# Hash-bucket attention and a feed-forward block: the hand-written order of 1185 steps is remade

## The chip, the cores and the metric

The kernel runs on one core of one Trainium2 chip. The metric is device time in microseconds (us) of one execution; where several runs are given, the median counts. A profiled execution has a time of its own, and inside it a span, from the first to the last instruction that the profiler saw.

## The reference

Inputs are q, k, v of shape (4 batches, 8 heads, 768 rows, 64), a projection of 64 x 6, a gain of 512, and two weight matrices, 512 x 2048 and 2048 x 512.

```python
q_bits = einsum('bhsd,dk->bhsk', q, proj) > 0      # k_bits likewise: 6 bits a row
mask   = q_bucket[:, :, :, None] == k_bucket[:, :, None, :]
scores = where(mask, q @ k.T / 8, -1e9)
attn   = softmax(scores);  a = attn @ v
x      = a with heads side by side                 # (4, 768, 512)
xn     = (x - mean) / sqrt(var + 1e-6) * g_ln
out    = x + relu(xn @ w_ch1) @ w_ch2
```

A row whose bucket no key shares takes the mean of v.

## The kernel before

**Tiles.** The 4 x 768 rows are cut into 12 units of 256 query rows (u = 0 to 11, three to a batch). A batch's 8 heads are two groups of four (g = 0, 1). A score step `S` (line 558) takes one unit, one group and one third of the keys (256 keys), so there are 72 steps s = 6u + 3g + third. A group's four heads lie at partitions 0, 32, 64, 96. Mask and scores are one accumulation: hash bits as +-0.5 are multiplied first (operand `G`), then q and k (`qb`, `kb`).

**What a step does.** `S.t.s` issues 24 matmuls on TensorE (PE) into two PSUM tiles `sc`, `E.a.s.0` and `E.a.s.1` (line 575) are the two exponentials on ScalarE (ACT), and `A.t.s` (line 587) multiplies their result with v and a column of ones into `acc`. `na`, `nb`, `nc`, `ag` on VectorE (DVE) turn `acc` into normalised rows and their mean and variance; `rs` on GpSimd (POOL) takes the root; `ce` centres; `fl` (line 638) transposes the rows by a DMA that SyncE (SP) issues. `F.t.u.p` (line 654) is one eighth of the first feed-forward product, `R` its relu on ACT or DVE, `P` (line 717) one of the seven products of a Strassen scheme for the second one, with its sums `ss` on DVE, `Y` adds a product to the rows and `O` stores a quarter of a unit.

**The first batch** (b = 0) has a path of its own, so as to start early. `lx` (line 370) loads a slab of q or k as it lies in memory. `tn.v.g.t.kp` (line 375, by `turn`, line 298) transposes one third kp of tensor t (0 is q, 1 is k) of group g; `ca` casts it to bf16; `ha.t.g.t.kp` (line 392) multiplies it in fp32 with the spread projection `pfull`, and `bh` (line 396) takes the signs into `G`. Thirds that aren't wanted at once take the way `hc`, `bc`, `sl`, `bi`. `lv` loads v, `cv` casts it into `vaug`, `sq` sums it and `sc` copies the sum. Unit 0 has no DMA transpose: `ft` transposes on PE and `fc` brings it out with the gain.

**Later batches** load with `LX` (line 507, after a one-column memset `gx` on POOL that holds the place), transpose with `tu`, cast with `CA`, hash with `hm` (line 521), take signs with `bt`, and go to DRAM and back (`mw` line 543, `mr` line 546) to reach the layout of `G`.

**Weights.** `lw1.p.n` (line 445) and `lw2.p.n` (line 456), n = 0 to 3, load a quarter of a weight matrix each, with a cast on the way, issued by POOL. `wg` multiplies the gain in for units from 1 on, `sw` forms Strassen's sums of weights.

**Warming.** `warm` (line 360) is 8 products of ones with ones, 512 columns each, into a PSUM tile of their own; `wm.t.0` to `wm.t.7` (line 365) are 8 more, one at a time, in the same tile. Nothing reads them.

**The order.** Nothing is scheduled by a compiler. `ORDER` (lines 16 to 136) lists 1185 words `name.engine.arguments`, and the loop at line 756 issues them as they stand. Each engine runs its own words strictly in that order; words of different engines meet only where one needs data or a buffer of another. The engine letter (v, a, p, s, t) says who does the step. `SLOTS` (lines 139 to 163) gives each tile its buffer by the order in which tiles are first named: `pp` has three double banks of PSUM for the pairs of `sc`, for `acc` and for the warming tile, `f` has two banks for everything else.

```python
for word in ORDER.split():
    name, eng, *args = word.split(".")
    OPS[name](ENGINES[eng], *map(int, args))
```

Of the kernel before, what the change touches and what calls it, by code (L numbers as in the profile page):

```python
# [21 lines left out]
tn.v.1.1.0 S.t.1.2 E.a.1.1 tn.v.1.0.0 ha.t.1.1.1 bh.v.1.1.1 cv.p.0.0.0 tn.v.1.1.2 gx.p.1.0.0 S.t.2.2  # L22
cv.p.0.0.2 cv.p.0.4.2 ca.p.1.1.2 E.a.1.0 ca.a.1.0.0 lv.s.1.0.3 lw1.p.1 ha.t.1.0.0 bh.v.1.0.0 gx.p.1.0.1
LX.s.1.0.0 ha.t.1.1.2 bh.v.1.1.2 E.a.2.1 lw1.p.0 ca.v.1.1.0 LX.s.1.0.1 tn.v.0.0.1 S.t.4.2 E.a.2.0
lv.s.1.0.2 ca.v.0.0.1 E.a.4.1 ha.t.1.1.0 A.t.0.2 A.t.2.2 sq.t.0.0 E.a.4.0 bh.v.1.1.0 S.t.3.2
sc.v.0.0 A.t.1.2 cv.a.0.4.0 E.a.3.1 hc.t.0.0.1 E.a.3.0 lw2.p.0 na.v.0.0 S.t.5.2 bc.v.0.0.1
sl.t.0.0.1 bi.v.0.0.1 E.a.5.1 sq.t.0.4 tn.v.1.0.1 S.t.8.2 hc.t.1.0.1 nb.v.0.0 nc.v.0.0 E.a.5.0
bc.v.1.0.1 E.a.8.0 A.t.4.2 A.t.5.2 sc.v.0.4 A.t.3.2 na.v.0.1 nb.v.0.1 E.a.8.1 sl.t.1.0.1
ca.a.1.0.1 bi.a.1.0.1 S.t.6.2 gt.t E.a.6.0 nc.v.0.1 ag.v.0.1 S.t.7.2 ag.v.0.0 ce.v.0.1
ft.t.0.1 ce.v.0.0 gc.v E.a.6.1 E.a.7.0 ft.t.0.0 S.t.9.2 E.a.7.1 E.a.9.0 fc.v.0.1  # L30
E.a.9.1 fc.v.0.0 F.t.0.3 A.t.7.2 R.a.0.3 F.t.0.7 R.a.0.7 S.t.10.2 tn.v.1.0.2 E.a.10.0
tu.v.1.0.1.2 gx.p.1.1.0 LX.s.1.1.0 lw1.p.2 tu.v.1.0.1.3 tu.v.1.0.0.3 lv.s.1.0.1 E.a.10.1 tn.v.0.0.2 hc.t.0.0.2
ca.a.0.0.2 tu.v.1.0.1.0 A.t.6.2 bc.v.0.0.2 sl.t.0.0.2 F.t.0.6 R.a.0.6 lw2.p.3 A.t.8.2 bi.v.0.0.2
# [24 lines left out]
A.t.25.2 O.s.1.0 R.a.2.6 nb.v.3.1 nc.v.3.1 F.t.2.4 nc.v.3.0 A.t.24.2 ag.v.3.0 su.p.2.0
A.t.26.2 na.v.4.0 E.a.29.1 LX.s.2.1.0 S.t.28.2 E.a.28.1 E.a.28.0 R.v.2.4 ag.v.3.1 hm.t.2.0
# [82 lines left out]
    E="012302132023132032103230103231032031230120302123031230120321013202120320",  # L142
# [646 lines left out]
```

## Time and profile before

| what | us |
|---|---|
| median of 3 runs | 295.62 (294.36 to 295.92) |
| the profiled execution | 294.86 |
| its span | 293.2 |
| DVE busy, mean of one relu (line 669) | 0.681 |
| ACT busy, mean of one relu (line 667) | 0.598 |
| first score matmul | 8.91 |
| last matmul ends | 288.9 |

The page gives, for each engine, its busy time; then the span in 40 slices; then the chain of work that ended last; then groups of equal instructions as `line engine operation out<-in xcount | busy, mean ns | idle before, what ended it`. A row of a timeline is `start us, length us, engine line operation out<-in xcount [idle before <-what ended it]`; rows with a count are runs of the same instruction. A row of the waits is `engine line <- what released it: us in total, times, longest`.

### The profile page before, as it was taken

Reading aid. Unit: us, or ns where it says so; the run is one execution under the profiler, and the core shown is the slowest. Engines: PE = TensorE matmul, PEld = TensorE weight load, DVE = VectorE, ACT = ScalarE, POOL = GpSimd, SP = SyncE. Lnnn points to the kernel's source line nnn. Section 1 sums busy time; section 2 is a strip of 40 time slices with the busy share of each in tenths; the row PEclk is TensorE's granted clock in tenths of the full one; section 3 lists DMA queues with packets and bytes.
Section 4 is the critical chain, followed back from the end, with each engine's and each line's share of the span. In section 5 each row is a group of like instructions: output and inputs, shape, how many; then the busy total and the mean of one; then the engine's idle time right before and its main releaser. Section 6 shows DMA issues by size and latency. Waiting matters only on the chain.

```text
span 293.2 us, 10524 instructions
## 1 busy us (share of the span) xinstructions
PE 285.6 (97%) x4650; PEld 227.7 (78%) x4650; DVE 206.8 (71%) x474; ACT 206.2 (70%) x236; POOL 54.0 (18%) x88
## 2 busy tenths in 40 slices
PE   8999999999999999999999999999999999999994
PEld 4677778648788887878778778877888878897883
DVE  4757899996769795797667995866666654773433
ACT  4689999998966978784865896887793694515240
POOL 5261325222423005000300107210010010000000
PEclk9999999999999999999999999999999999999999
DMA  6999997747744692362330352230410402304022
GB/s 223 302 319 250 216 277 133 139 134 171 174 122 131 134 307 76 127 189 51 98 82 1 83 132 63 60 61 3 92 37 2 74 2 52 78 6 104 2 72 73
DMA packets 31055, 34.10 MB, mean 116 GB/s; under 512 B 15521, under 2 KB 27809, under 8 KB 31010
## 3 DMA queue, kind: packets, MB, share of 16 engines
q1 hardware_dynamic: 25938, 28.72, 35.6%
q0 software_dynamic: 4224, 4.19, 8.9%
q8 instruction: 36, 0.59, 0.9%
q10 hardware_dynamic: 848, 0.53, 0.7%
q14 instruction: 9, 0.07, 0.1%
HBM read 27.86 MB, written 6.88 MB: 118 GB/s over the span
## 4 chain that ended last, share of the span: by engine, by line
PE 91%; DMA 3%; DVE 2%; SPq 1%; ACT 1%; issue 0%; ACTq 0%; DVEq 0%
PE f L659 27%; PE sc L570 18%; PE X L725 13%; PE acc L595 12%; PE Yb L725 7%; PE hp L526 3%; PE Ya L725 3%; PE hf L394 3%; PE f L674 2%; PE warm L363 1%; ACT E L576 1%; DMA G<-Bd 1%; DMA Bd<-B 1%; PE warm L366 1%; DMA xnT<-xc 1%; SPq L547 1%
## 5 line engine op out<-in xcount | busy, mean ns | idle before, releaser
L576 ACT ACTIVATE E<-sc,bias_sb 128x1024 bf16<-128x1024 f32 x144 | 153.1, 1111 | 36.0 <-PE sc L570 32.6
L659 PE MATMUL f<-xnT,w_sb 128*128 128x256 bf16 x768 | 94.2, 273 | 0.7 <-DMA xnT<-xc 0.6
L659 PEld LDWEIGHTS <-w_sb 128*128 128x128 bf16 x768 | 71.4, 98 | 13.6 <-issue 5.7
L667 ACT ACTIVATE hb<-f 128x512 bf16<-128x512 f32 x67 | 39.6, 598 | 34.5 <-PE f L659 34.5
L570 PE MATMUL sc<-qb,kb 32*128 32x256 bf16 x1152 | 52.5, 267 | 0.0
L595 PEld LDWEIGHTS <-E 128*128 128x128 bf16 x1152 | 40.8, 98 | 4.0 <-issue 2.5
L595 PE MATMUL acc<-vaug,E 128*128 128x65 bf16 x1152 | 43.7, 194 | 0.1
L570 PE MATMUL sc<-G 6*128 6x256 bf16 (+1 forms) x576 | 42.7, 273 | 1.1 <-ACT E L576 0.8
L725 PEld LDWEIGHTS <-hb 128*128 128x128 bf16 x352 | 33.4, 98 | 5.4 <-issue 1.3
L570 PEld LDWEIGHTS <-kb 32*128 32x128 bf16 x1152 | 30.5, 93 | 1.5
L635 POOL TENSOR_SCALAR rs<-mv 128x2 f32<-128x2 f32 x12 | 3.3, 277 | 150.4 <-DVE mv L624 150.4
L730 DVE TENSOR_TENSOR x<-X,x 128x256 f32<-128x256 f32 x44 | 18.4, 419 | 16.5 <-PE X L725 16.3
L570 PEld LDWEIGHTS <-G 6*128 6x128 bf16 (+1 forms) x576 | 16.0, 91 | 16.7 <-issue 13.3
L725 PEld LDWEIGHTS <-S 128*128 128x128 bf16 x264 | 25.0, 98 | 4.8 <-issue 1.4
L669 DVE TENSOR_SCALAR hb<-f 128x512 bf16<-128x512 f32 x29 | 19.7, 681 | 12.0 <-PE f L659 11.8
L304 DVE STREAM_TRANSPOSE T<-X 128x384 f32<-128x384 f32 (+2 forms) x52 | 26.1, 535 | 0.0
L725 PE MATMUL Yb<-w_sb,S 128*128 128x256 bf16 x176 | 22.9, 273 | 0.0
L608 DVE SCALAR_TENSOR_TENSOR y<-vsB,acc 128x520 f32<-128x520 f32 x24 | 16.5, 689 | 8.1 <-PE acc L595 7.8
L725 PE MATMUL X<-wt,hb 128*128 128x256 bf16 x168 | 21.8, 273 | 0.0
L617 DVE TENSOR_TENSOR x<-y,rc 128x512 f32<-128x512 f32 x24 | 17.8, 742 | 0.8
L621 DVE BATCH_NORM_STATS2 st<-x 128x6 f32<-128x256 f32 x48 | 17.4, 412 | 0.2
L730 DVE TENSOR_TENSOR x<-Yb,x 128x256 f32<-128x256 f32 x22 | 9.2, 420 | 9.5 <-PE Yb L725 9.5
(95 smaller groups left out, 268.3 us busy)
## 6 DMA issues: line engine op xcount, KB each, us to landing
out_dram<-x SPq DMA_DIRECT2D x45, 128.0 KB
X<-in_k_dram SPq DMA_DIRECT2D x7, 768.0 KB
vn<-in_v_dram SPq DMA_DIRECT2D x24, 192.0 KB
X<-in_q_dram SPq DMA_DIRECT2D x6, 768.0 KB
w_sb<-in_moe_w_ch_dram POOLq DMA_DIRECT2D x8, 512.0 KB, 10.8
vn<-in_v_dram SPq DMA_DIRECT2D x2, 768.0 KB
X<-in_q_dram SPq DMA_DIRECT2D x2, 512.0 KB
Bd<-B SPq DMA_DIRECT2D x6, 96.0 KB
```

Source lines behind the costliest of these rows:

```text
L304: nc.vector.transpose(d[:, j], s[:, j, kj0 : kj0 + n])
L570: nc.tensor.matmul(sc(s, i // 2)[:, i % 2, 256 * kk : 256 * kk + 256], lh, rh, start=(rep == 0), stop=(rep == 2), skip_group_check=True,)
L576: nc.scalar.activation(E(s)[:, heads(h)], sc(s, h), AF.Exp, scale=EXP_SCALE, bias=bias_sb)
L595: nc.tensor.matmul(acc[:, qt, (D + 1) * i : (D + 1) * (i + 1)], E(s)[:, i, 256 * kk + P * qt : 256 * kk + P * qt + P], vaug(u // 3)[:, 4 * ...
L608: nc.vector.scalar_tensor_tensor(yt(u, g), vs, EPS_ROW, made[f"acc{u}{g}"][:, :, :A], op0=AOP.mult, op1=AOP.add,)
L617: nc.vector.tensor_tensor(xo, a[:, :, :, 0:D], rc.to_broadcast([P, 2, 4, D]), op=AOP.mult)
L621: nc.vector.bn_stats(stats(u)[:, qt, g], xt(u)[:, qt, 256 * g : 256 * g + 256])
L659: nc.tensor.matmul(f1[:, n].rearrange("p (t x) -> p t x", t=2), w1_sb[:, dt, P * nt : P * nt + P], xnT(u)[:, :, dt], start=(dt == 0), stop ...
L667: nc.scalar.activation(hb(u)[:, 2 * p : 2 * p + 2], f1, AF.Relu)
L669: eng.tensor_scalar_max(hb(u)[:, 2 * p : 2 * p + 2], f1, 0.0)
L725: nc.tensor.matmul(f2, lh[:, n], rh[:, n], start=(first and n == 0), stop=(n == 7), skip_group_check=True)
L730: nc.vector.tensor_tensor(x, made[f"{prod(u, k)}{u}"], x, op=AOP.add)
```

## The change

Both `ORDER` and `SLOTS` are replaced; no other line differs. The words are the same 1185 steps, with the same count on PE (4650 matmuls) and SP; some change engine: 9 relus go from ACT to DVE (ACT 67 to 58, DVE 29 to 38), the gain on weight quarter 0 from ACT to DVE, the casts `CA` from DVE to ACT (2) and POOL (1), two casts of v from ACT and DVE to POOL, two sums' copies from DVE to ACT, one `bi` and, net, one `ca` from ACT to DVE and POOL.

In the first scores the order of PE is

```
before: warm  wm.0 wm.1 wm.2 wm.3  ha.0.1.0 ha.0.0.0  wm.7 wm.5 wm.4  S.0  ha.0.1.1 ha.0.1.2  wm.6
        S.1  ha.1.1.1  S.2  ha.1.0.0 ha.1.1.2  S.4  ha.1.1.0  A.0 A.2 sq.0.0  S.3 ...
after:  warm  ha.0.0.0 ha.0.1.0  wm.2 wm.1 wm.4  S.0  ha.0.1.1 ha.0.1.2  wm.5 wm.7 wm.3
        S.1  ha.1.0.0  wm.0 wm.6  S.2  ha.1.1.1 ha.1.1.0  S.4  ha.1.1.2  sq.0.0  A.0 A.2  gt  S.3 ...
```

On POOL the weight loads stand so, with what stands between them:

```
before: on.0 sel p32 on.1  lw1.3  pmem ca.0.1.1 ca.1.1.1 cv.0.0.0 gx cv.0.0.2 cv.0.4.2 ca.1.1.2  lw1.1
        gx  lw1.0 lw2.0  gx  lw1.2 lw2.3  gx  lw2.1  rs.0 CA su  lw2.2
after:  on.0 p32 on.1 pmem sel ca.0.1.0 ca.0.1.1 gx cv.0.0.2 ca.1.1.1  lw1.1 lw1.3  ca.1.1.2  lw1.0
        cv.0.4.0 gx  lw1.2 lw2.0  gx  lw2.2 lw2.1  gx  lw2.3  rs.0 CA ...
```

The core of the diff, its first words and its last units:

```diff
@@ first scores
-lg.s on.p.0 mem.v tab.a pf.v warm.t wm.t.0 wm.t.1 wm.t.2 wm.t.3
-sel.p tn.v.0.0.0 p32.p tn.v.0.1.0 on.p.1 lw1.p.3 ca.a.0.0.0 pmem.p ha.t.0.1.0 bh.v.0.1.0
-ha.t.0.0.0 ca.a.0.1.0 bh.v.0.0.0 wm.t.7 wm.t.5 wm.t.4 tn.v.0.1.1 ca.p.0.1.1 tn.v.0.1.2 S.t.0.2
-E.a.0.0 E.a.0.1 ha.t.0.1.1 bh.v.0.1.1 ha.t.0.1.2 bh.v.0.1.2 wm.t.6 tn.v.1.1.1 ca.p.1.1.1 ca.a.0.1.2
+lg.s on.p.0 mem.v tab.a pf.v warm.t tn.v.0.0.0 p32.p on.p.1 pmem.p
+sel.p tn.v.0.1.0 ca.v.0.0.0 ha.t.0.0.0 bh.v.0.0.0 ha.t.0.1.0 bh.v.0.1.0 ca.p.0.1.0 wm.t.2 wm.t.1
+tn.v.0.1.1 ca.p.0.1.1 wm.t.4 tn.v.0.1.2 tn.v.1.0.0 S.t.0.2 ha.t.0.1.1 bh.v.0.1.1 ha.t.0.1.2 bh.v.0.1.2
+E.a.0.1 wm.t.5 E.a.0.0 wm.t.7 wm.t.3 ca.a.0.1.2 gx.p.1.0.0 S.t.1.2 tn.v.1.1.2 LX.s.1.0.0
+cv.p.0.0.2 ha.t.1.0.0 tn.v.1.1.1 ca.a.1.0.0 E.a.1.0 wm.t.0 wm.t.6 cv.v.0.0.0 E.a.1.1 S.t.2.2
...
@@ units 9 to 11
-Y.v.9.5 Y.v.9.7 nc.v.11.1 P.t.9.3 Y.v.9.3 P.t.9.4 Y.v.9.4 O.s.9.3 O.s.9.0 O.s.9.2
-F.t.10.6 R.a.10.6 ag.v.11.1 F.t.10.1 O.s.9.1 ag.v.11.0 rs.p.11 ce.v.11.0 fl.s.11.0 F.t.10.0
-R.a.10.1 R.a.10.0 F.t.10.5 R.a.10.5 F.t.10.4 F.t.10.3 R.a.10.4 R.a.10.3 ce.v.11.1 fl.s.11.1
+na.v.11.1 F.t.10.7 R.a.10.7 P.t.9.6 nb.v.11.1 Y.v.9.6 P.t.9.5 nc.v.11.1 Y.v.9.5 ag.v.11.1
+ag.v.11.0 P.t.9.7 rs.p.11 Y.v.9.7 P.t.9.3 Y.v.9.3 P.t.9.4 F.t.10.4 R.a.10.4 ce.v.11.0
+fl.s.11.0 Y.v.9.4 F.t.10.3 F.t.10.6 R.a.10.3 R.a.10.6 F.t.10.2 ce.v.11.1 fl.s.11.1 O.s.9.2
...
@@ SLOTS
-    X="0123023120312032",
+    X="0123021302130213",
-    pp="0121020102011202102102102121021020...",
+    pp="0122120120212012021012102120102102...",
```

More of the change, by code (lines that the diff above doesn't have):

```diff
@@ new lines @@
+R.v.6.5 ss.v.6.1 fl.s.7.1 P.t.6.2 A.t.54.2 ss.v.6.2 ss.v.6.4 sc.a.3.0 P.t.6.1 A.t.56.2
+E.a.57.0 ss.v.6.3 Y.v.6.2 Y.v.6.1 E.a.57.1 S.t.59.2 E.a.59.1 F.t.7.5 na.v.9.0 ag.v.8.1
+R.v.7.5 rs.p.8 P.t.6.6 S.t.60.2 E.a.60.0 Y.v.6.6 P.t.6.5 Y.v.6.5 P.t.6.7 E.a.60.1
+Y.v.6.7 P.t.6.3 Y.v.6.3 P.t.6.4 cv.p.3.4.2 E.a.59.0 Y.v.6.4 O.s.6.0 O.s.6.2 S.t.61.2
+A.t.59.2 F.t.7.1 R.v.7.1 E.a.61.0 nb.v.9.0 O.s.6.1 su.p.3.4 sp.t.3.4 A.t.57.2 sc.a.3.4
+nc.v.9.0 E.a.61.1 A.t.58.2 F.t.7.6 F.t.7.0 R.a.7.6 S.t.64.2 E.a.64.0 R.v.7.0 F.t.7.7
```

227 lines of the change are left out of this document (110 added, 117 removed).

## The prediction

> **What bounds the kernel now.** I read the page's head and chain first, to see which engine carries the end; then the waits of PE; then the stretches, to see where PE is not full.
>
> ```profile
> span 293.2 us, 10524 instructions
> PE 285.6 (97%) x4650; PEld 227.7 (78%) x4650; DVE 206.8 (71%) x474; ACT 206.2 (70%) x236; POOL 54.0 (18%) x88
> PE 91%; DMA 3%; DVE 2%; SPq 1%; ACT 1%; issue 0%; ACTq 0%; DVEq 0%
> w_sb<-in_moe_w_ch_dram POOLq DMA_DIRECT2D x8, 512.0 KB, 10.8
> ```
> ```profile
> PE sc L570 <- ACT E L576: 0.8, 3, 0.4
> PE f L659 <- DMA xnT<-xc: 0.6, 1, 0.6
> PE sc L570 <- DMA G<-Bd: 0.3, 1, 0.3
> PE ft L644 <- DVE xc L628: 0.2, 1, 0.2
> ```
> ```profile
> 0.00:7.00 7.00, 5.89 (x15) 2.67 (x16) 3.00 (x18) 3.09 (x4) 4.01 (x20) 1.00 0.67 214
> 7.00:14.00 7.00, 7.00 (x77) 4.62 (x79) 4.96 (x14) 4.34 (x6) 2.17 (x2) 1.00 1.11 298
> 22.00:29.00 7.00, 6.59 (x160) 5.34 (x160) 5.17 (x15) 6.82 (x9) 0.97 (x2) 1.00 1.07 251
> 29.00:36.00 7.00, 6.27 (x133) 4.72 (x132) 6.38 (x18) 6.78 (x9) 2.36 (x6) 1.00 1.02 205
> 60.00:120.00 60.00, 60.00 (x1048) 46.52 (x1047) 47.69 (x102) 48.78 (x54) 15.84 (x19) 1.00 0.58 155
> 130.00:265.00 135.00, 135.00 (x2195) 111.87 (x2192) 93.63 (x209) 91.65 (x103) 15.13 (x23) 1.00 0.25 60
> ```
>
> PE carries 91% of the chain. The stretches give PE busy in their third column: full for 60 of 60 us and 135 of 135 us. There the same 4650 matmuls in another order cannot get shorter; they can only acquire holes. What can be won lies at the start (22 to 36 us: 14 us with 12.86 busy, and ACT at 13.60 of 14, so exponentials pace PE), and in the two waits for DMA, one each near 128 us and 269 us. No row of PE's waits names a weight load: w_sb is never late in the kernel before, so issuing all weights early removes no wait of its own.
>
> **The change part by part.** Every step is still issued once. Nine relus go from ACT to DVE, where one takes 0.681 instead of 0.598 us; neither engine is full past 60 us (48.78 and 47.69 of 60), so with PE as cover I cost them at nothing; uncovered they would be 9 x 0.68 = 6.1 us of DVE.
>
> *The first score.* Its parts in the kernel before, on PE, DVE and ACT:
>
> ```profile
> 1.11 3.60 PE L363 MATMUL warm<-ones 128*128 128x512 bf16 x8 [1.11 <-DVE bias_sb L320]
> 4.50 1.91 PE L366 MATMUL warm<-ones 128*128 128x512 bf16 x4
> 6.21 2.12 PE L394 MATMUL hf<-tp,pfull 128*128 128x256 f32 x8
> 8.16 0.81 PE L366 MATMUL warm<-ones 128*128 128x512 bf16 x3
> 8.91 0.29 PE L570 MATMUL sc<-G 32*128 32x256 bf16 x4
> 9.67 1.99 PE L394 MATMUL hf<-tp,pfull 128*128 128x256 f32 x8
> ```
> ```profile
> 4.34 1.66 DVE L304 STREAM_TRANSPOSE tp<-X 128x256 f32<-128x256 f32 x4 [1.21 <-DMA X<-in_q_dram]
> 7.50 0.42 DVE L307 TENSOR_SCALAR G<-hf 128x256 bf16<-128x256 f32 x1 [1.51 <-PE hf L394]
> 8.37 0.48 DVE L307 TENSOR_SCALAR G<-hf,hrow 128x256 bf16<-128x256 f32 x1 [0.44 <-PE hf L394]
> 8.77 1.41 DVE L304 STREAM_TRANSPOSE tp<-X 128x256 f32<-128x256 f32 x4
> ```
> ```profile
> 5.14 0.63 ACT L311 ACTIVATE qb<-tp 128x512 bf16<-128x512 f32 x1 [1.76 <-DVE tp L304]
> 6.03 1.08 ACT L311 ACTIVATE kb<-tp 128x512 bf16<-128x512 f32 x1 [0.26 <-DVE tp L304]
> 9.78 2.12 ACT L576 ACTIVATE E<-sc,bias_sb 128x1024 bf16<-128x1024 f32 x2 [2.66 <-PE sc L570]
> 28.29 6.14 ACT L576 ACTIVATE E<-sc,bias_sb 128x1024 bf16<-128x1024 f32 x6
> 35.62 1.11 ACT L576 ACTIVATE E<-sc,bias_sb 128x1024 bf16<-128x1024 f32 x1 [0.23 <-PE sc L570]
> ```
>
> Before, the hash products begin at 6.21, behind four warming products, and q's comes second. In the changed order q's comes first and needs only the q transposes, done at about 5.1 (ACT's cast of them starts at 5.14). Four fp32 products take about 1.0 us at full pace (8 in 1.99). Started at 5.2, with the first half at half pace (warming products are 0.43 us apart before 6.2, then 0.22, as the seven of L366 show), the first group ends near 6.5, the second near 7.4; its signs follow 0.2 behind and take 0.42, so the first score starts at 8.1, not 8.91: 0.8 us sooner. The q cast, now on DVE, and the k cast, now on POOL, are done by about 7.2, so they don't delay it.
>
> Five warming products instead of one now stand behind the first score: 4 x 0.22 = 0.9 us more of PE. On PE alone that takes the 0.8 back. But ACT is the tighter one here. One exponential costs 1.0 us of a run (6 in 6.14). From the first one to the last of step 9, ACT now has 20 exponentials (20.1), two k casts (2.0), two q casts (1.1), a v cast (0.8) and a sum's copy (0.4): 24.4 us from 9.0, so 33.4 if it never waits; before, that point is 34.43 (28.29 + 6.14). Following the words of PE and DVE by hand I find ACT waiting about 0.8 us, at steps 8 and 6 (their `sc` banks come free when `na` has read `acc`), so 34.2, and the exponential of step 10 at 35.2 instead of 35.62. I take **-0.5** for the start; ends: -1.1 (no wait of ACT) and the loss under the rivals.
>
> *The loads.*
>
> ```profile
> 15.20 0.83 POOL L475 CAST vaug<-vn 128x768 bf16<-128x768 f32 x1 [1.23 <-DMA vn<-in_v_dram]
> 18.86 0.83 POOL L475 CAST vaug<-vn 128x768 bf16<-128x768 f32 x1 [2.03 <-DMA vn<-in_v_dram]
> 20.66 0.80 POOL L446 DMA_DIRECT2D w_sb<-in_moe_w_ch_dram  x1
> ```
>
> One weight quarter, 512 KB, is issued ahead of the hash before; now none is until both k casts and a v cast are through on POOL. At 298 GB/s (7 to 14 us) 512 KB are 1.7 us, so the v loads that landed at 15.20 and 18.86 should land near 13.5 and 17.1. POOL then issues the first two quarters near 14.5 and the last near 25; with 10.8 us to landing the one for unit 0's first product is there by 26, against its use at about 33. The later batch's q, k and v loads share the DMA engines with all eight; DMA is near 1.0 busy until 36 us before, too, and batch 1 is hashed at about 41. I cost this at nothing; its cover is those 7 us and more.
>
> *The hash of batch 2 and the last unit.*
>
> ```profile
> 119.71 2.61 DMA Bd<-B
> 125.50 3.16 DMA G<-Bd
> 128.70 0.84 PE sc L570 x23
> ```
> ```profile
> 262.91 3.07 SPq L744 DMA_DIRECT2D out_dram<-x  x4
> 266.09 2.51 SPq L639 DMA_TRANSPOSE xnT<-xc  x2
> 264.20 1.00 DVE L630 TENSOR_SCALAR xc<-x,mv,rs 128x512 bf16<-128x512 f32 x2 [1.13 <-POOL rs L636]
> 267.39 2.48 DMA xnT<-xc
> ```
>
> Between `hm.t.2.1` and the first score that needs it stand, by PE's own paces, 9.3 us of work before and 14.1 after: the 0.3 us wait goes. At the end, the two transposes of unit 11 stand in SP behind four output stores and start at 266.09, though the first half was ready at about 264.75. In the new order all four stores come behind them; they start up to 1.3 us sooner, more than the 0.6 us that PE waits. Past 60 us the nearest distances between a score and the use of its exponentials (2.61 us at least, in both orders) and between users of a PSUM bank are no shorter than before, so I see nothing late next: **-0.9**.
>
> Sum: -0.5 - 0.3 - 0.6 = -1.4: span 291.8, the profiled execution 294.86 - 1.4 = 293.5. The median of the runs is 0.76 above that execution; I keep that distance: **294.2 us**.
>
> [...] The clock shows only in the spacing: 0.43 us between warming products until 6.2, 0.22 from 7.9 on, after PE had been busy without a break from 1.11. In the changed order PE falls idle at 4.71 until about 5.2.
>
> [...]
>
> **The rivals.**
>
> [...]
>
> *A DVE step waits for a load in its turn.* `tn.v.1.0.0` now stands ahead of the signs for step 1, and `cv.v.0.0.0` ahead of the signs for step 4. DVE reaches the first at 9.5; that slab was used without a wait at 13.38 before, so it lands somewhere up to 13.4 or, without the weight load, 11.7. Up to 10.5 it is free (ACT has casts to do until 12.65); each us later costs one, 1.2 to 2.9 at the ends, in place of the -0.5: 295.9 to 297.6. It is the fourth load that SP issues, before any of v, which speaks for the early end.
>
> *ACT never waits, or PE's start packs better*: -1.1 to -2.5 at the start, as the 1.14 us of PE's idling there and the 2.66 before the first exponential allow: 292.2 to 293.6.
>
> *The weight loads do nothing and the two late waits stay* (the change doesn't do what it says): 295.1 to 295.6.
>
> **How the numbers follow.** Forecast 0.40 (own range 293.4 to 295.0), clock later 0.20, load wait 0.23, better start 0.13, nothing 0.04. 0.5% is 1.48 us, about what a measurement of this kernel can tell from no change: below 294.14 is faster, above 297.1 slower. Faster: half of the forecast's 0.40 and the better start, 0.33. Slower: two thirds of the load wait (its price may be paid twice, at both places) and a fifth of the clock's, 0.19. Same: 0.48. The range, 292.6 to 297.3, leaves out the outer halves of the better start and of the load wait.
>
> **What would show it.** [...] A DVE row `tp<-X` with an idle time put down to DMA near 9.5: the load wait. The exponential of step 10 near 35.2. No `xnT<-xc` and no `G<-Bd` among PE's waits. PE full from 60 to 265; a hole there, or a wait for `w_sb`, would make the prediction wrong.

## The result and the profile after

| | before | after |
|---|---|---|
| median of 17 runs | 295.27 (292.74 to 297.46) | 296.93 (296.58 to 299.98) |
| profiled execution | 294.86 | 298.64 |
| its span | 293.2 | 296.6 |
| first score matmul | 8.91 | 7.76 |

The ratio is 1.0095, interval 1.0068 to 1.0122: the change costs 0.95%, where the prediction's 294.2 was to be 0.5% less.

The after runs fall into two groups. Ten have a mean granted clock of 1.000 and lie at 296.58 to 297.17 (median 296.65). Seven have 0.988 to 0.993 and lie at 297.84 to 299.98 (median 298.64). The profiled execution is one of the seven, so its trace shows a loss that not every run has. The ten at full clock still lie 1.4 above the median of before. The kernel before has a clock of 0.994 or less too, but more rarely: in 8 of the 128 runs of it that were taken beside the experiments.

From the page of after: the span, the busy times, the clock granted in 40 slices, the chain's shares, the weight loads.

```profile
span 296.6 us, 10514 instructions
PE 286.5 (97%) x4650; PEld 229.4 (77%) x4650; DVE 214.9 (72%) x482; ACT 201.0 (68%) x224; POOL 58.1 (20%) x92
PEclk9999799999999999999999999999999999999999
PE 90%; DVE 3%; DMA 3%; ACT 1%; SPq 1%; issue 0%; POOL 0%; DVEq 0%; ACTq 0%
w_sb<-in_moe_w_ch_dram POOLq DMA_DIRECT2D x8, 512.0 KB, 19.3
```

The waits of PE in after, then its stretches (length, then busy time of PE, PEld, DVE, ACT, POOL, then granted clock, DMA share, GB/s):

```profile
PE vp L487 <- DVE hb L669: 1.6, 1, 1.6
PE sc L570 <- ACT E L576: 1.6, 2, 1.3
PE sc L570 <- DVE G L307: 0.5, 1, 0.5
PE sc L570 <- DVE y L608: 0.4, 1, 0.4
PE ft L644 <- DVE xc L628: 0.2, 1, 0.2
```
```profile
7.00:14.00 7.00, 6.47 (x71) 3.91 (x70) 5.20 (x15) 5.05 (x6) 2.56 (x5) 1.00 1.04 359
22.00:29.00 7.00, 6.13 (x160) 4.78 (x160) 4.31 (x11) 6.39 (x7) 0.90 (x3) 1.00 1.15 299
29.00:36.00 7.00, 5.40 (x109) 3.81 (x109) 6.50 (x18) 5.96 (x7) 1.59 (x2) 0.79 1.11 311
60.00:120.00 60.00, 58.38 (x1034) 44.95 (x1031) 52.42 (x110) 46.58 (x51) 10.98 (x15) 1.00 0.58 160
130.00:265.00 135.00, 135.00 (x2234) 111.77 (x2233) 99.37 (x215) 90.13 (x99) 22.25 (x30) 1.00 0.27 61
```

Three things are to be seen. The two late waits of before, `xnT<-xc` and `G<-Bd`, are gone. A new wait of 1.6 us, of `vp` for a relu `hb` on DVE, stands in their place, and PE is no longer full between 60 and 120 us (58.38). And from 29 to 36 us PE has 5.40 busy us at a mean clock of 0.79, where before it had 6.27 at full clock.

To say how much each place costs I took, for each step on PE, the time from its first matmul to that of the next step, less what the same pair takes where PE is dense (a score step 0.77 us, a product `F` 0.87, a product `A` 0.49). What is left over is waiting or half clock; the four warming products that now stand behind the first score are work, about 0.9 us, and not in it. Its sums by stage, worked out from the traces, in us:

| trace | to the first score | to step 9 | to step 13 | steps 20 to 28 | steps 36 to 41 | last two units | all stages |
|---|---|---|---|---|---|---|---|
| before | 1.04 | 3.49 | 0.55 | 0.26 | 0.42 | 1.23 | 7.66 |
| after | 0.77 | 5.37 | 1.88 | 1.90 | 0.05 | 0.49 | 11.08 |

The difference is 3.42, the difference of the spans 3.4. The late waits gave back 0.37 and 0.74, as predicted. The losses are 1.9 before step 9, 1.3 just behind it, and 1.6 at 77 us. The rows of each:

*The start*, on PE and on DVE:

```profile
4.70 2.48 PE L394 MATMUL hf<-tp,pfull 128*128 128x256 f32 x8
7.02 0.81 PE L366 MATMUL warm<-ones 128*128 128x512 bf16 x3
7.76 0.29 PE L570 MATMUL sc<-G 32*128 32x256 bf16 x4
11.70 0.29 PE L570 MATMUL sc<-G 32*128 32x256 bf16 x4 [0.53 <-DVE G L307]
```
```profile
10.56 0.77 DVE L304 STREAM_TRANSPOSE tp<-X 128x256 f32<-128x256 f32 x2 [1.58 <-DMA X<-in_q_dram]
```

The hash products follow the eight warming products without a gap, at 4.70, and the first score comes at 7.76. But DVE then waits 1.58 us for q's slab of the other group, with the signs for step 1 behind that wait, and step 1 starts at 11.70 against 11.81: of 1.15 us won 0.11 are left.

*Unit 0*, the exponentials on ACT and the normalisation on DVE:

```profile
12.56 2.12 ACT L576 ACTIVATE E<-sc,bias_sb 128x1024 bf16<-128x1024 f32 x2 [0.30 <-PE sc L570]
14.85 2.12 ACT L576 ACTIVATE E<-sc,bias_sb 128x1024 bf16<-128x1024 f32 x2 [0.17 <-PE sc L570]
22.07 4.23 ACT L576 ACTIVATE E<-sc,bias_sb 128x1024 bf16<-128x1024 f32 x4 [0.87 <-PE sc L570]
27.21 2.12 ACT L576 ACTIVATE E<-sc,bias_sb 128x1024 bf16<-128x1024 f32 x2 [0.39 <-PE sc L570]
29.95 4.21 ACT L576 ACTIVATE E<-sc,bias_sb 128x1024 bf16<-128x1024 f32 x4 [0.62 <-PE sc L570]
34.57 2.12 ACT L576 ACTIVATE E<-sc,bias_sb 128x1024 bf16<-128x1024 f32 x2 [0.41 <-PE sc L570]
38.63 1.11 ACT L576 ACTIVATE E<-sc,bias_sb 128x1024 bf16<-128x1024 f32 x1 [0.72 <-PE sc L570]
```
```profile
30.64 0.41 DVE L430 CAST G<-hf 128x256 bf16<-128x256 f32 x1
31.20 0.49 DVE L628 TENSOR_SCALAR xc<-x,mv 128x512 bf16<-128x512 f32 x1
31.60 0.42 DVE L313 TENSOR_SCALAR qb<-tp 128x512 bf16<-128x512 f32 x1
31.94 0.48 DVE L628 TENSOR_SCALAR xc<-x,mv 128x512 bf16<-128x512 f32 x1
```

ACT now waits for PE's scores (in the trace of before it does so once between its first exponential and step 9, for 0.70 us), so PE paces this stage and not ACT. Two steps for batch 1 (a bias `G`, a cast `qb`) lie in the middle of unit 0's chain on DVE. The exponential of step 10 starts at 38.63, before at 35.62.

*77 us*, on DVE, POOL and PE:

```profile
73.68 0.55 DVE L630 TENSOR_SCALAR xc<-x,mv,rs 128x512 bf16<-128x512 f32 x1 [0.35 <-POOL rs L636]
74.14 0.68 DVE L699 TENSOR_TENSOR wt<-w_sb,wt 128x1024 bf16<-128x1024 bf16 x1
74.74 2.15 DVE L630 TENSOR_SCALAR xc<-x,mv,rs 128x512 bf16<-128x512 f32 x1
76.82 1.21 DVE L699 TENSOR_TENSOR wt<-w_sb,wt 128x1024 bf16<-128x1024 bf16 x1
77.95 1.28 DVE L669 TENSOR_SCALAR hb<-f 128x512 bf16<-128x512 f32 x2
```
```profile
74.81 1.81 POOL L480 TENSOR_TENSOR t<-vn 128x768 f32<-128x768 f32 x1 [1.17 <-DMA vn<-in_v_dram]
76.69 0.79 POOL L481 TENSOR_TENSOR t<-t 128x256 f32<-128x256 f32 x1
```
```profile
78.69 0.28 PE L487 MATMUL vp<-vsum,ones 128*128 128x256 bf16 x1 [1.62 <-DVE hb L669]
```

The same two DVE operations stand there twice: 0.55 and 0.68 us alone, 2.15 and 1.21 us while POOL adds. The relus behind them are late, and PE with them.

### The profile page after: what moved, and what is told of

Same layout as the page of the kernel before. It is cut to its first block, busy times and chain, and to the rows that moved or that the text cites. A ratio compares the mean times of both kernels' runs of the same rounds, so it can differ in the third digit from the quotient of the medians.

```text
span 296.6 us, 10514 instructions
## 1 busy us (share of the span) xinstructions
PE 286.5 (97%) x4650; PEld 229.4 (77%) x4650; DVE 214.9 (72%) x482; ACT 201.0 (68%) x224; POOL 58.1 (20%) x92
## 4 chain that ended last, share of the span: by engine, by line
PE 90%; DVE 3%; DMA 3%; ACT 1%; SPq 1%; issue 0%; POOL 0%; DVEq 0%; ACTq 0%
PE f L659 28%; PE sc L570 18%; PE X L725 13%; PE acc L595 12%; PE Yb L725 7%; PE Ya L725 3%; PE hp L526 3%; DMA X<-in_q_dram 3%; PE f L674 2%; ACT E L576 1%; PE hf L394 1%; DVE xc L630 1%; SPq L373 1%; DVE wt L699 1%; PE vp L494 0%
## 5 line engine op out<-in xcount | busy, mean ns | idle before, releaser
L659 PE MATMUL f<-xnT,w_sb 128*128 128x256 bf16 x768 | 93.2, 273 | 0.0
L570 PE MATMUL sc<-qb,kb 32*128 32x256 bf16 x1152 | 53.5, 269 | 0.1
L667 ACT ACTIVATE hb<-f 128x512 bf16<-128x512 f32 x58 | 34.2, 597 | 26.0 <-PE f L659 23.7
L595 PEld LDWEIGHTS <-E 128*128 128x128 bf16 x1152 | 41.9, 98 | 4.0 <-issue 2.6
L595 PE MATMUL acc<-vaug,E 128*128 128x65 bf16 x1152 | 44.6, 194 | 0.0
L725 PEld LDWEIGHTS <-hb 128*128 128x128 bf16 x352 | 32.7, 98 | 6.3 <-issue 2.7
L669 DVE TENSOR_SCALAR hb<-f 128x512 bf16<-128x512 f32 x38 | 25.6, 682 | 15.4 <-PE f L659 15.3
L630 DVE TENSOR_SCALAR xc<-x,mv,rs 128x512 bf16<-128x512 f32 x22 | 14.8, 696 | 0.4 <-POOL rs L636 0.4
```

Source lines behind the costliest of these rows:

```text
L570: nc.tensor.matmul(sc(s, i // 2)[:, i % 2, 256 * kk : 256 * kk + 256], lh, rh, start=(rep == 0), stop=(rep == 2), skip_group_check=True,)
L595: nc.tensor.matmul(acc[:, qt, (D + 1) * i : (D + 1) * (i + 1)], E(s)[:, i, 256 * kk + P * qt : 256 * kk + P * qt + P], vaug(u // 3)[:, 4 * ...
L630: nc.vector.tensor_scalar(xc(u)[:, t], xt(u)[:, t], mv(u)[:, t, 0:1], rstd(u)[:, t : t + 1], op0=AOP.subtract, op1=AOP.mult,)
L659: nc.tensor.matmul(f1[:, n].rearrange("p (t x) -> p t x", t=2), w1_sb[:, dt, P * nt : P * nt + P], xnT(u)[:, :, dt], start=(dt == 0), stop ...
L667: nc.scalar.activation(hb(u)[:, 2 * p : 2 * p + 2], f1, AF.Relu)
L669: eng.tensor_scalar_max(hb(u)[:, 2 * p : 2 * p + 2], f1, 0.0)
```

## The experiments

Theory after the traces: the change wins what was predicted at its start and its end, and loses more in three places: in the order of DVE and PE up to unit 0's normalisation, in the clock, which is halved for 3.4 us near 33 us, and at 77 us, where DVE's steps take 2.15 and 1.21 us beside POOL's additions. Rivals: the early weight loads hold up other loads; the late relus come from the words ahead of them and not from POOL; the clock falls for a reason outside the kernel. Diffs are in words of `ORDER`; each kernel is the changed one unless it says otherwise. "Step 9 behind the first score" is the distance between those two scores: 22.38 us before, 25.04 after.

**1. The relus ahead of the weight sums at 77 us.**

```diff
- ce.v.2.0 fl.s.2.0 sw.v.4.1 ce.v.2.1 ... F.t.1.4 sw.v.4.0 ... R.v.1.4 R.v.1.2
+ ce.v.2.0 fl.s.2.0 ce.v.2.1 ... F.t.1.4 ... R.v.1.4 R.v.1.2 sw.v.4.1 sw.v.4.0
```

> Changed kernel with the two weight sums sw.4 put behind the two relus R.1.4 and R.1.2 on VectorE; nothing else. Theory A (a VectorE step stretched by GpSimd's sums of v, with relus queued behind it, makes TensorE wait 1.6 us at 77 us): that wait goes, about 1.7 us less than the changed kernel, near 295.2 us. Theory B (the loss is all in the first 37 us): no difference, 296.5 to 297.5.

Measured: 296.74, ratio 1.0059 [1.0032, 1.0085]. The wait of `vp` is gone, 0.6 us of another (`f` for the copy `vsB` on DVE) has come, and steps 20 to 28 cost 0.98 instead of 1.90. So the place is right and half of it can be mended by the order; why DVE is late at all is left to run 10. The median stays above the 295.2 that theory A expected; the seven runs with a clock of 0.998 or more have a median of 296.09.

**2. Without the five late warming products.**

```diff
- E.a.0.1 wm.t.5 E.a.0.0 wm.t.7 wm.t.3 ... E.a.1.0 wm.t.0 wm.t.6
+ E.a.0.1 E.a.0.0 ... E.a.1.0
```

> Changed kernel without the five warming products that stand behind the first score (nothing reads them). Theory A (TensorE is the tighter engine up to score step 3, so warming there is paid): 0.5 to 1.1 us less than the changed kernel, 295.8 to 296.4. Theory C (ScalarE is the tighter engine there, as I predicted): no difference. If they hold the clock up, a lower granted clock in more executions and a longer time.

Measured: 296.91, ratio 1.0069 [1.0039, 1.0099]. The score of step 1 starts at 11.80, since DVE waits for the load anyway (1.96 us at 10.66), and step 9 comes 24.73 behind the first score instead of 25.04. By the span's own time step 9's scores start at 32.24 instead of 32.80, and the six runs with a clock of 0.997 or more have a median of 296.24, against 296.65. So of PE's 1.1 us of warming 0.3 to 0.6 are paid: less than theory A at its full price, but not nothing, as theory C had it.

**3. A shorter chain on DVE for unit 0.**

```diff
- bi.v.1.0.1 S.t.6.2 E.a.8.1 ... ft.t.0.1 ca.v.1.0.1 ce.v.0.0 fc.v.0.1 ft.t.0.0 fc.v.0.0
+ S.t.6.2 E.a.8.1 bi.a.1.0.1 ... ft.t.0.1 ce.v.0.0 fc.v.0.1 ft.t.0.0 fc.v.0.0 ca.v.1.0.1
```

> Changed kernel with two VectorE steps taken out of unit 0's way to its first product: one copy of bits goes to ScalarE, one q cast stands behind the two gains. Theory A (TensorE idles 1.5 us ahead of the transposes of unit 0 since VectorE is 0.8 us longer there, and that idling lets the clock fall): first product of unit 0 about 0.8 us sooner, fewer executions with a clock under 1.0, median 295.5 to 296.3. Theory B' (the weight loads issued early delay the start): no difference.

Measured: 298.78, ratio 1.0125 [1.0081, 1.0168]. Nothing is won: PE's scores of step 7 still wait 1.26 us for an exponential, and ACT has one step more. Step 9 comes 24.13 behind the first score, but q's slab landed early in this trace; run 6, with the two steps in their old places and the slab as early, has 24.15. The two DVE steps in the chain are not what paces it. That part of the theory falls.

**4. The signs ahead of the transposes that wait for a load.**

```diff
- tn.v.0.1.2 tn.v.1.0.0 S.t.0.2 ha.t.0.1.1 bh.v.0.1.1 ha.t.0.1.2 bh.v.0.1.2
+ tn.v.0.1.2 S.t.0.2 ha.t.0.1.1 bh.v.0.1.1 ha.t.0.1.2 bh.v.0.1.2 tn.v.1.0.0
```

> Changed kernel with the transposes of the second q group put behind the signs for score steps 1 and 2, as in the kernel before. Theory A (that step waits 1.6 us for its load and holds up the signs and score step 1): score step 1 starts 0.6 us sooner, near 11.1, and the total is 0 to 0.6 us less than the changed kernel. Theory C (ScalarE has casts to do until 12.6 anyhow): score step 1 sooner, total the same.

Measured: 297.69, ratio 1.0084 [1.0051, 1.0117]. Step 1 comes 3.34 us behind the first score instead of 3.93, so the load's wait cost 0.6 there, and step 9 comes 24.44 behind it, 0.6 sooner. The median doesn't show it: 7 of 11 runs had a clock of 0.993 or 0.994 (median 298.5), the other four lay at 296.13 to 296.68. The traces up to here show the halved clock in four of five of the changed order's kernels, always for exactly 3.413 us and always behind a stretch in which PE idles. That called for runs on the clock itself.

**5. Filling PE's hole, first try.** Eight products of 192 columns behind the scores of step 7, in columns of a PSUM tile that nothing reads; the bias step of that tile stands behind them (lines of this kernel from 402 on are shifted by one).

```diff
- bi.v.1.0.1 S.t.6.2 ... ag.v.0.1 S.t.7.2
+ S.t.6.2 ... S.t.7.2 fill.t.0 ... fill.t.7 ... bi.v.1.0.1 ag.v.0.1
```

> The changed kernel with eight products of 192 columns, whose results nothing reads, put on PE behind the scores of step 7, where PE idles for 1.5 us around 31 us; the normalisation's bias step and its first aggregate stand behind them. Theory A (the clock is halved at about 33 us because PE is too little busy in the 3.4 us ahead of it): every run, the profiled one too, has a granted clock of 1.000, and the median falls to that of the changed kernel's own runs at full clock, 296.65, though the products themselves cost up to 0.6 us where they reach past the hole. Theory B (the drop has another cause, such as heat or power): about 4 runs in 10 still show 0.988 to 0.993, the profile may show half clock from about 33 to 36.4 us, and the median is that of the changed kernel or 0.6 above it.

Measured: 302.15, ratio 1.0238 [1.0206, 1.0270]; every run had a clock of 0.994 or less. PE and DVE in this kernel:

```profile
31.12 0.40 PE L571 MATMUL sc<-G 32*128 32x256 bf16 x2 [1.25 <-ACT E L577]
32.52 1.46 PE L402 MATMUL hf<-ones 128*128 128x192 bf16 x8
```
```profile
34.02 0.42 DVE L431 CAST G<-hf 128x256 bf16<-128x256 f32 x1 [3.29 <-PE hf L402]
```

My edit made its own damage: the products ran behind the clock's fall, and DVE's whole normalisation waited 3.29 us for them, so PE idled more and the clock stayed at half for 10.2 us. It can't speak for theory B, and it shows what such a hole costs when it grows.

**6. The second weights' loads later.**

```diff
- hc.t.1.0.1 lw2.p.0 ... lw2.p.2 lw2.p.1 ... lw2.p.3 ... rs.p.0 S.t.12.2
+ hc.t.1.0.1 ... rs.p.0 lw2.p.0 lw2.p.2 lw2.p.1 lw2.p.3 S.t.12.2
```

> The changed kernel with its four loads of the second weights issued about 15 us later, behind the first unit's last reciprocal on POOL, as late as before. Theory A (the loss is PE's wait for unit 0's normalisation on DVE at 31 us, and for DVE's steps at 77 us): nothing changes, ratio to the kernel before 1.007 to 1.012, and both waits stand in the trace. Rival C (the weight loads share the DMA engines with the first loads of q, k and v and make them late): the transposes of the second batch no longer wait at 10.6 us, and the time falls by 1 us or more.

Measured: 297.50, ratio 1.0083 [1.0051, 1.0115]: not faster. In its profile q's slab landed sooner (DVE goes on at 9.96 after 0.88 us of waiting), but that is ahead of any weight load (the first is issued at 14.16, in after at 14.78), and it landed at either time in other kernels too. The half clock stands at 77.55 in this trace instead of near 33. The rival of the weight loads falls.

**7. The kernel before, with only the stores of chunk 9 behind the last transposing loads.**

```diff
- Y.v.9.4 O.s.9.3 O.s.9.0 O.s.9.2 F.t.10.6 ... O.s.9.1 ... ce.v.11.1 fl.s.11.1
+ Y.v.9.4 F.t.10.6 ... ce.v.11.1 fl.s.11.1 O.s.9.3 O.s.9.0 O.s.9.2 O.s.9.1
```

> The kernel before, with the four output stores of chunk 9 moved behind the last unit's second transposing load on SP, and nothing else. My prediction's term for the end of the change, alone: the 0.6 us of PE's wait for the load of xnT near 269 us goes and nothing is late next, so 0.6 us less, ratio 0.998. Rival (the stores, issued later, are late in their turn at the end, or the load still waits for its source): 1.000 or more, with the wait or a longer tail behind the last product.

Measured: 294.25, ratio 0.9969 [0.9942, 0.9995]. The waits of PE and the rows of SP's queue:

```profile
PE sc L570 <- DMA G<-Bd: 1.2, 1, 1.2
PE f L659 <- DMA xnT<-xc: 0.2, 1, 0.2
```
```profile
264.93 2.50 SPq L639 DMA_TRANSPOSE xnT<-xc  x2
267.48 1.97 SPq L744 DMA_DIRECT2D out_dram<-x  x4
```

The transposes start at 264.93 instead of 266.09 and the wait falls from 0.6 to 0.2. Four moved words on the old kernel are a gain; this term of the prediction was right by itself. The other late wait is still there, and it is 1.2 us in this trace against 0.3 before, with nothing changed ahead of it: its size differs from execution to execution.

**8. The kernel before, with four warming products behind the first hash products.**

```diff
- warm.t wm.t.0 wm.t.1 wm.t.2 wm.t.3 ... ha.t.0.0.0
+ warm.t ... ha.t.0.0.0 wm.t.0 wm.t.1 wm.t.2 wm.t.3
```

> The kernel before, with four warming products moved behind the first group of hash products, and nothing else: the change's start alone. By the theory that the start gains (the first score comes sooner since the hash products no longer stand behind warming ones): the hash products begin at 5 us or sooner, the first score at 8.2 to 8.6, and the time falls by 0.3 to 0.7 us, ratio 0.998. By the theory that what the start wins is lost again on PE and DVE before unit 0's normalisation is done: the first score comes sooner but the one of step 9 not, and the ratio is 1.000 to 1.003. A later clock would show as hash products at 0.43 us each up to about 9 us.

Measured: 297.88, ratio 1.0071 [1.0037, 1.0104]. PE in the profiled execution (301.52):

```profile
5.55 3.78 PE L394 MATMUL hf<-tp,pfull 128*128 128x256 f32 x8 [0.84 <-DVE tp L304]
9.12 2.24 PE L366 MATMUL warm<-ones 128*128 128x512 bf16 x7
```

Here full clock does come later: a gap of 0.84 us behind the warming products, all eight hash products at half pace (3.78 us instead of 2.12), the clock full from 10.26 only. Its runs reach from 295.52 to 301.67 and the profiled one is among the three longest, near 301.5, so not every run pays this in full; no trace shows what the other eight, at 295.52 to 299.24, lose against before. In the traces of the changed order the gap is 0.45 us at most (run 9) and the clock is full by 7.11 at the latest (run 5); that the shorter gap is the reason is likely, not shown.

**9. Products for the hole, that nothing waits for.** Eight of 256 columns, behind step 7's scores, in the tile of `bi.v.1.0.1`, which keeps its place.

```diff
- ag.v.0.1 S.t.7.2 E.a.6.0
+ ag.v.0.1 S.t.7.2 fill.t.0 ... fill.t.7 E.a.6.0
```

> The changed kernel with eight bf16 products of 256 columns and 128 rows added on PE behind the scores of step 7, in the hole ahead of unit 0's transposes; no step waits for them but the next user of their PSUM buffer, and their results are read by nothing. In the traces so far each 3.413 us window of the clock after which it was halved had streamed at most 0.36 of 8192 columns (a score counted at its 32 of 128 rows, fp32 twice), and each window with 0.39 or more kept the clock; in the changed kernel the window ahead of the drop has 0.31. Theory A (too few columns in one window halve the clock): these products add 2048 columns, 0.25, so no run shows a granted clock under 0.997, and the median is 296.4 to 296.9, with none of the runs near 298.6. Theory B (the drop comes of something else): 4 of 10 runs stay at 0.988 to 0.993.

Measured: 299.19, ratio 1.0128 [1.0083, 1.0174]; four of six runs at 0.987 to 0.994. As stated, theory A failed. PE in this kernel:

```profile
30.89 0.28 PE L570 MATMUL sc<-G 32*128 32x256 bf16 x2 [1.25 <-ACT E L576]
32.01 1.89 PE L749 MATMUL hf<-ones 128*128 128x256 bf16 x8
```

The hole lies inside step 7's scores, whose second half waits for an exponential, so products behind these scores can't fill it. The window ahead of the clock's fall, 27.81 to 31.22, has 0.32 of the columns, and the products start 0.8 us behind its end. So my edit missed the window, as run 5's did, and the run leaves open whether a fuller window keeps the clock; run 13 tests it.

**10. POOL's additions held back.** A copy of one column, written by the relu R.v.1.2, into a scratch column on POOL.

```diff
- R.v.1.4 R.v.1.2 O.s.0.3
+ R.v.1.4 R.v.1.2 dl.p O.s.0.3
```

> The changed kernel with one tiny copy on POOL, of a column that the relu R.v.1.2 writes, ahead of the sums of the values of batch 1, heads 4 to 7, so that POOL's three additions start only when DVE is through with the steps that they lay beside at 75 to 78 us. Theory A (DVE's step of 2.15 instead of 0.54 us is stretched by POOL's addition beside it): the xc step is back at 0.5 to 0.7 us, the wait of PE's vp for DVE's relu (1.6 us) goes or falls under 0.4, and the time falls by 1.2 to 1.8 us. Rival (the relus come late because the weight sums and the centring stand ahead of them, whoever runs beside): the wait stays over 1 us.

Measured: 295.64, ratio 1.0034 [1.0009, 1.0059]. DVE and POOL in this kernel:

```profile
72.84 0.54 DVE L630 TENSOR_SCALAR xc<-x,mv,rs 128x512 bf16<-128x512 f32 x1
73.30 0.69 DVE L699 TENSOR_TENSOR wt<-w_sb,wt 128x1024 bf16<-128x1024 bf16 x1
```
```profile
75.75 1.82 POOL L480 TENSOR_TENSOR t<-vn 128x768 f32<-128x768 f32 x1
```

The same DVE words in the same order take 0.54 and 0.69 us, and steps 20 to 28 cost 0.11 instead of 1.90. One instruction on POOL, which only makes it wait, takes away the whole loss at 77 us: DVE's steps were long because POOL's additions lay beside them.

**11. Four edits together**: 9's products, 10's copy, 4's order of the signs, and the gains behind step 3.

```diff
- tn.v.1.0.0 S.t.0.2 ... A.t.2.2 gt.t gc.v S.t.3.2
+ S.t.0.2 ... bh.v.0.1.2 tn.v.1.0.0 ... A.t.2.2 S.t.3.2 gt.t gc.v
```

> The changed kernel with four edits: the products in the hole of unit 0, POOL's additions held back to 78 us, the transposes of batch 1's query slab behind the signs that they held up, and the transposed gains (gt, gc) behind the scores of step 3. If the three losses that the traces show (0.9 us at 10.6 us, 1.8 us of clock where it comes, 1.6 us at 77 us) are the whole reason why the change didn't gain, this falls to 293.3 to 294.3, ratio 0.993 to 0.997: the start and the two late waits are won and nothing is lost. If it stays over 295.3, a loss that I haven't named is left in the first 40 us.

Measured: 295.00, ratio 1.0007 [0.9979, 1.0034]: level with the kernel before. Seven runs lay at 293.98 to 295.06, five, with a clock of 0.992 or 0.993, at 296.24 to 296.76. The seven have a median of 294.10, inside the expected 293.3 to 294.3, with three of them above it; in the other five the clock wasn't held.

**12. The kernel before with both late waits mended**: 7's edit, and batch 2's hash moved up.

```diff
- F.t.3.7 R.a.3.7 F.t.3.0 tu.v.2.1.1.0 ... tu.v.2.1.1.2 hm.t.2.1 ... bt.v.2.1 mw.s.2.1 mr.s.2.1.1 mr.s.2.1.3
+ tu.v.2.1.1.0 ... tu.v.2.1.1.2 hm.t.2.1 bt.v.2.1 mw.s.2.1 mr.s.2.1.1 mr.s.2.1.3 F.t.3.7 R.a.3.7 F.t.3.0
```

> The kernel before with the stores of chunk 9 behind the last unit's transposing load (as in the run of that alone) and the hash of batch 2's second half, with its transposes, bits and loads, ahead of the products of unit 3 that it stood behind: the two late waits of my prediction, without the new start. By the prediction's terms 0.6 + 0.3, and by the trace in which the wait at 128 us was 1.3 us up to 1.9: ratio 0.994 to 0.997, no row G<-Bd in PE's waits. Rival (DVE's transposes, five in a row, hold up the steps behind them): a new wait of PE for DVE of 0.5 us or more near 115 us, ratio 0.998 or more.

Measured: 296.90, ratio 1.0076 [1.0051, 1.0101]. The rival it was, from the waits of PE:

```profile
PE hp L526 <- DVE T L304: 1.9, 1, 1.9
```

`G<-Bd` is gone and a wait of 1.9 us for five transposes in a row on DVE has come. This trace, of one of the longest runs (298.55), also has 1.5 us of idle PE at 45.74 for which the profile names no releaser, so not all of its loss is that rival's.

**13. Products on both sides of the hole.** Kernel 11 with six more ahead of step 6.

```diff
- sl.t.1.0.1 gx.p.1.1.1 bi.v.1.0.1
+ sl.t.1.0.1 fill.t.100 ... fill.t.105 gx.p.1.1.1 bi.v.1.0.1
```

> The combined kernel (products in the hole, POOL's additions held back, the query slab's transposes behind the signs, the gains behind step 3) with six more products of 256 columns, whose results nothing reads, on PE ahead of the scores of step 6. Theory A (a 3.413 us window with at most 0.36 of 8192 columns streamed halves the clock): these add 0.19 on the near side of the hole, so that no window between 24 and 35 us stays under 0.40 whatever the phase; no run under a granted clock of 0.997 (the combined kernel had 5 of 12 at 0.992 or 0.993), and the median falls to that of its undisturbed runs or to 0.4 us above it, 294.1 to 294.6, ratio 0.997 to 0.999. Theory B (the drop comes of something else): 4 of 10 runs stay at 0.992 to 0.994 and 296.5.

Measured: 294.87, ratio 0.9999 [0.9982, 1.0017]. All twelve runs have a clock of 0.996 or more and lie within 294.34 to 295.37; the group at 296.5 is gone. More work on PE, none of it useful, held the clock in these twelve. It costs about 0.8 us against kernel 11's undisturbed runs (median 294.10), about twice the 0.4 that was allowed for at most.

**14. One k cast on DVE.** Kernel 11 with `ca.a.1.1.0` as `ca.v.1.1.0`.

```diff
- E.a.2.1 ca.a.1.1.0 bh.v.1.0.0
+ E.a.2.1 ca.v.1.1.0 bh.v.1.0.0
```

> The combined kernel with one cast of k (batch 1, first third), 1.1 us of ACT between the exponentials of steps 2 and 4, on DVE as in the kernel before. Theory A (ACT's casts between the exponentials push back steps 4 and 3 and so unit 0's normalisation): the exponentials of step 4 begin 0.8 to 1.1 us sooner, PE's waits between the first score and step 9 fall from 4.7 by 0.5 to 1.0 us. Rival (PE's own products, warming ones among them, and the chain of values on DVE pace steps 4 to 9): under 0.3 us.

Measured: 295.04, ratio 1.0009 [0.9988, 1.0030]. The exponentials of step 4 begin 8.92 us behind the first one, in kernel 11 8.60; waits up to step 9 are 5.19, in kernel 11 4.74. ACT's cast is not the cause.

**15. All of these**: kernel 13 with 14's cast and without the late warming products.

```diff
- E.a.0.1 wm.t.5 E.a.0.0 wm.t.7 wm.t.3 ... wm.t.0 wm.t.6 ... ca.a.1.1.0
+ E.a.0.1 E.a.0.0 ... ca.v.1.1.0
```

> The run with products on both sides of the hole, the k cast on DVE and none of the five late warming products. If the losses named so far are the whole, everything that the change wins is kept: 293.0 to 293.9, ratio 0.993 to 0.996, as good as or better than the kernel before with only its stores moved (0.997). If it is above 294.5, something in the first 40 us is not understood.

Measured: 295.08, ratio 1.0006 [0.9986, 1.0026]. Above 294.5, so by its own expectation something was left. The chain of this trace runs through the eight products behind step 7 (0.98 us) and 0.78 us of `gt`.

**16. The gains later**, alone on the changed kernel (the PSUM buffers renumbered to suit).

```diff
- A.t.2.2 gt.t gc.v S.t.3.2 ... sl.t.1.0.1 ... ce.v.0.1
+ A.t.2.2 S.t.3.2 ... sl.t.1.0.1 gt.t ... ce.v.0.1 gc.v
```

> The changed kernel with the eight small products of the gains (gt) behind the bits of step 6's keys instead of ahead of the scores of step 3, and their copy (gc) behind the first centring. Theory A (they stand on the path there, since PE goes straight from products to scores with ACT waiting): the scores of step 3 start 0.5 to 0.6 us sooner and everything up to unit 0's transposes with them; 0.5 us less in the runs at full clock, 296.65 to 296.1. Rival (PE waits for ACT's exponentials there anyway): step 3 no sooner than 0.2, the time unchanged.

Measured: 297.15, ratio 1.0059 [1.0040, 1.0078]. Step 3 comes 12.38 us behind the first score, in the changed kernel 13.06: theory A's 0.5 to 0.6 is there. But seven of eight runs had a clock of 0.985 to 0.994; the one at 1.000 took 296.24, where 296.1 was expected. Its trace has half clock for two windows, from 29.78 to 36.60. Why it falls more often here isn't shown: PE's longest wait for an exponential is not longer than in after, 1.2 against 1.3 us.

**17. All that was settled**: 10's copy, 4's order, no late warming, 16's gains, and seven products that hold the clock, four ahead of step 6 and three ahead of step 7.

```diff
- sl.t.1.0.1 ... S.t.7.2
+ sl.t.1.0.1 fill.t.100 ... fill.t.103 gt.t ... fill.t.0 fill.t.1 fill.t.2 S.t.7.2
```

> The changed kernel with all that the runs have settled: POOL's additions held back, the query slab's transposes behind the signs, no late warming products, the gains later, and seven products of 256 columns that keep the clock, four ahead of the scores of step 6 and three ahead of those of step 7, not behind them. No clock under 0.996, no wait near 77 us; PE's waits from the first score to step 9 fall from 5.3 or 6.0 to 4.5 or less if the gains and the place of the products were what is left: 293.3 to 294.3, ratio 0.994 to 0.998. If it stays at 295, that part of the loss lies in the new start itself, spread over many small waits, and stays open.

Measured: 294.17 (293.53 to 294.66), ratio 0.9965 [0.9951, 0.9978], all twelve runs with a clock of 0.996 or more. From its waits of PE and its stretches:

```profile
PE sc L570 <- ACT E L576: 1.5, 3, 0.7
PE hf L749 <- DVE G L430: 0.7, 1, 0.7
```
```profile
60.00:120.00 60.00, 60.00 (x1062) 46.87 (x1060) 50.59 (x110) 47.50 (x52) 11.97 (x17) 1.00 0.57 153
```

PE is full from 60 to 120 us again. This kernel beats both, as does kernel 7; it stands at 23.27 us between the first score and step 9, still 0.9 above before. Its own seven products are part of that: they take about 0.11 us each, and the three ahead of step 7 wait 0.7 us for DVE first; how much of it is paid isn't shown.

## Why the prediction was wrong

**The first score: right, and too careful.** It was put at 8.1, with an idle gap of PE ahead of it; it came at 7.76 with none. Part of the 1.15 us is luck of the two traces. Full clock came at 6.66 in the trace of before and at 5.72 in that of after; in the other traces the first score comes at 8.12 (run 7) and 8.30 (run 12) with the old start, and at 7.31 to 8.42 with the new one. A late full clock at the start (*clock later* among the chances: 0.20, a fifth of it counted as slower) didn't come here, and no run shows what it would cost the changed order: in the traces of that order the clock is full by 7.11 at the latest. Run 8, the old kernel with four warming products moved, shows a late one: full clock at 10.26, the first score at 11.30 instead of 8.91, 1.7 us of it in the hash products alone (3.78 instead of 2.12).

**"But ACT is the tighter one here": wrong.** On this rested the -0.5. ACT was to wait 0.8 us up to step 9; in the trace it waits about 2.8 (0.30, 0.17, 0.87, 0.39, 0.62 and 0.41, each for a score). I had counted ACT's work and added PE's by hand, but PE waits in its turn for DVE. The sentence that I had set aside, that on PE alone the late warming takes the 0.8 back, was nearer to it. The exponential of step 10 was foretold at 35.2 and came at 38.63. Shown of these 3.4 us are 0.6 for the load (run 4), about 0.6 for the gains (run 16: in the changed order they stand where PE paces) and 0.3 to 0.6 for the late warming products (run 2), all up to step 9. Half clock behind it makes 1.4: from step 9's scores to the exponential of step 10 it is 5.8 us in after and 4.4 in runs 4 and 10, whose traces are at full clock there. The DVE steps in unit 0's chain and ACT's cast are ruled out (runs 3, 14). What makes the remaining 0.2 to 0.5 us is not settled. The -0.5 was also more than its own working gave: 34.43 to 34.2 and 35.62 to 35.2 are 0.2 and 0.4.

**The load in DVE's turn: a rival that came in beside the forecast.** It was "free up to 10.5", and q's slab came at 10.56. Since the first score was sooner than foretold, DVE was there sooner too and the wait cost 0.6. I had treated it as all or nothing, with a price for a later load, and not seen that a better start raises the price. That the measured 296.93 lies inside the stated range, and inside this rival's 295.9 to 297.6, is luck: most of the loss came from places that had no price.

**The clock at 33 us: not among the rivals.** I looked at the clock only where it starts. Its price is 2.0 us between the two groups of after's runs. Runs 13, 15 and 17 show that PE's work near the hole decides it: none of their 36 runs is under 0.996, while 7 of 24 are in runs 11 and 14, which lack the products ahead of the hole.

**"I see nothing late next": wrong, at 77 us.** The step costed nine relus and the whole middle at nothing since neither engine was full past 60 us. That is an average. Run 10 shows the loss whole: 1.8 us, because POOL's three additions now fall on the steps that the relus stand behind. The trace of before had the pattern for all to see, and I didn't quote it:

```profile
45.98 1.89 DVE L617 TENSOR_TENSOR x<-y,rc 128x512 f32<-128x512 f32 x1
```
```profile
45.51 1.81 POOL L480 TENSOR_TENSOR t<-vn 128x768 f32<-128x768 f32 x1 [5.97 <-DMA vn<-in_v_dram]
```

The same DVE step takes 0.69 us at 28.21 in that trace. There it stretched a step that nothing waited for; the new order put one there that PE waits for.

**The two late waits: right**, 0.37 and 0.74 for 0.3 and 0.6, and run 7 has the second alone. The first was sized from one trace; in those of runs 7 and 8, whose order there is the old one, it is 1.2. Run 12 shows that it can't be had by moving the hash alone, as it was moved there.

**The weight loads: right.** No step waits for `w_sb`, and later loads change nothing (run 6).

## What to carry to other kernels

When an order is changed far from a wait, look through the trace for steps that take longer than their kin, find what ran beside them, and ask which step will lie there next. A stage where two engines alternate need not be paced by the one with the larger sum; follow what each wait ends on, and price a wait for a load against the start that you forecast, not the old one. And count the TensorE work of each few microseconds, not only its idle time: on a kernel this full, the loss of full clock cost 2.0 us, more than the 1.4 that the change was forecast to win.

## What the runs showed of the hardware

**In these traces the clock fell behind windows with few columns streamed.** Once full clock is granted, it changed in all 19 traces at multiples of 3.413 us from that point. I counted for each window the columns that PE's matmuls stream, each matmul by its start (a score, which uses 32 of 128 rows, as a quarter; fp32 twice), as a share of 8192, a round figure near what fits in at full pace (the 512-column products of line 674 start 0.216 us apart in before, which gives 8090 in 3.413 us). Of 1564 windows at full clock that end ahead of the last matmul nine were followed by half clock; they have 0.31, 0.32, 0.33 (three), 0.34 (two) and 0.36 (two). Of the 1555 others one has 0.35, and none else is under 0.377. Neither simpler count separates them: by the profile PE is busy for 50 to 81% of the nine and for as little as 45% of a window that kept the clock, and with a score counted as a whole the nine have 0.88 to 1.23, while windows down to 0.38 kept it. In after, that window is 29.61 to 33.02 with 0.31, though by the profile PE is busy for 57% of it (1.96 of 3.41 us), and the clock of the next 3.41 us is 0.50: with its scores counted whole the window has 0.88. In before, the lowest window has 0.39. Behind such a fall half clock went on after windows of up to 0.41 and ended after those of 0.44 and more. At the start of a kernel this doesn't separate: full clock came behind windows of 0.38 to 0.50, and in run 5 a window of 0.44 wasn't enough. Full clock first comes at 3.83 to 10.26 us in these traces, so the windows' edges lie elsewhere in each; that this is why one kernel has both kinds of runs is likely, not shown. A few matmul records may be missing (the page of run 8 has 4648 of 4650), so the shares are lower bounds.

**DVE's and POOL's steps were longer side by side.** In after, an fp32 to bf16 step of 0.54 us took 2.15 us beside a POOL addition of 1.81 us and ended 0.27 us behind it; a two-input DVE step of 0.68 took 1.21 beside one of 0.79. The other way round, POOL's next addition took 1.05 us beside that DVE step, and 0.73 in run 10. With POOL held back both DVE steps had their usual length (run 10). Not every DVE step beside POOL is longer: in run 10 the addition of 1.82 us lies beside a transpose of 0.57 and a copy of 0.39, which take 0.56 and 0.38 in after.
